# Seven block products over pairs of token tiles in the projections of a linear-attention kernel, and a planned order of the other engines

## The chip, the cores and the metric

The kernel runs on one core of a Trainium2 chip. The metric is the device time of one execution in microseconds; smaller is better. Five engines work side by side, each through its own list of instructions in order: PE (TensorE, matrix products into PSUM banks), DVE (VectorE), ACT (ScalarE), POOL (GpSimd) and SP, which here only issues DMA transfers. An instruction waits on semaphores for what it reads, and for the last reader of what it overwrites.

## The reference

For 2048 tokens of 640 channels, the kernel computes

```
out = x + attention(layernorm(x)) + mlp(layernorm(x))       S = 2048, D = 640
q, k, v   = split(xn @ wqkv)                 32 heads of 20
phi(z)    = [softmax(z @ w_phi), softmax(-z @ w_phi)]        per head, 40 wide
kv, z     = sum over tokens of phi(k)^T v, phi(k)
attention = ((phi(q) kv) / (phi(q) z + 1e-6)) @ wo
mlp       = gelu(xn @ w1 + b1) @ w2 + b2      640 -> 1728 -> 640
```

All of it is float32. The products `q @ w_phi` and `k @ w_phi` are folded into the weights before the projections start, so that one matrix `wkv` (640 x 1344 columns) gives the arguments of the feature maps of k (columns 0 to 639) and of q (640 to 1279), and 64 columns of v; `wv` (512 columns) gives the rest of v.

## The kernel before

A float32 operand is kept as two parts, `hi` (rounded to float32r, a form that PE reads at full speed) and `lo` (the remainder), and a product is three matmuls, hi·hi, hi·lo and lo·hi. ACT writes `hi`, and DVE or POOL subtracts it for `lo` (`split`, L60 and L63).

PE goes through four stages: the MLP of token blocks 0 and 1 (a block is 512 tokens), with the folding of the weights and the transposing of x beside it; the projections of 16 token tiles of 128; the MLP of blocks 2 and 3 with the attention's output beside it; and the end. The change is in the second, and in what runs beside the first.

**A tile of the projections** takes four banks' worth of products (`proj(t, i)`, matmuls at L913): columns 0 to 511 (i = 0), 512 to 1023 (i = 1), the "narrow" bank of 320 columns (i = 2: the last q columns and 64 of v) and the "wide" bank of v (i = 3). Each is five contraction chunks of 128, three matmuls a chunk: 15 matmuls. Three PSUM banks (0 to 2) take turns. The other five hold the sums over all tokens of phi(k)^T v; `kv_tile` (L974, L978, 11 short matmuls) adds the products of tile t-2 to them behind the first bank of tile t. The last of them, of tile 15, stands in the MLP that follows: `last_kv` puts it behind ten steps of that MLP, and these are the 30 matmuls of its first layer for weight chunks 0 and 1. The last order is `TAIL`: both tiles' banks 0 and 1 first, then narrow and wide of 14 and of 15.

**A feature map** (`features`, `k_tile`, `q_tile`; once for k and once for q of each tile) is a chain over three engines: ACT copies the bank to SBUF (L925), DVE takes maximum and minimum per head (L932, L933), POOL makes two differences (L938), ACT the exponentials of both (L939), DVE the sums (L941) and their reciprocals (L947, for q L991), and POOL the product with them (L949 for k, 128x1280; L992 and L995 for q). For k, ACT and DVE then split it (L60, L63: `lo` on DVE, 128x1280) for the products with v; for q, DVE turns it in blocks of 32 (L1001) and SP stores it. v itself goes from its bank to SBUF on ACT (L965, hi) and DVE (L967, lo).

**The order.** PE's list is written out by hand everywhere. In the MLP of blocks 0 and 1 the lists of all engines are as written; the call `order.close()` at L888, ahead of the projections, ends that, and from there the framework's scheduler decides the order in the lists of DVE, ACT, POOL and SP by its own estimates.

Weights of the output (`wo`) are split beside tiles 1, 2, 3, 6 and 7, and the first weights of the next MLP stage beside tiles 12 to 15, on ACT and POOL.

The kernel already has a product by seven blocks instead of eight elsewhere: in the MLP of blocks 2 and 3 (`cross`), which is not changed.

## Time and profile before

| | |
|---|---|
| median of 3 runs | 700.8 us (700.64 to 700.96) |
| profiled execution: its time, its span | 701.24 us, 699.5 us |
| PE busy | 693.6 us, 3331 matmuls |
| DVE, ACT, POOL busy | 523.3, 365.2, 437.9 us |
| MLP of blocks 0 and 1 | span 0 to 211 us |
| projections | 211 to 428 us |
| from there to the last product of `kv_tile` | 428.0 and 436.1 us |

The profiled execution is one of its own and took 0.44 us more than the median of the runs; the 1.74 us between its time and its span lie before the first and behind the last instruction that the profile shows. All times in the trace count from the span's start. A bare matmul of 128x512 here means 512 columns moved through PE with a 128x128 weight. PE is the engine to look at first, since it is busy 99% of the span; the other three have room on the average, but each feature map passes through all of them in turn.

### The profile page before, as it was taken

Reading aid. Unit: us, or ns where it says so; the run is one execution under the profiler, and the core shown is the slowest. Engines: PE = TensorE matmul, PEld = TensorE weight load, DVE = VectorE, ACT = ScalarE, POOL = GpSimd, SP = SyncE. Lnnn points to the kernel's source line nnn. Section 1 sums busy time; section 2 is a strip of 40 time slices with the busy share of each in tenths; the row PEclk is TensorE's granted clock in tenths of the full one; section 3 lists DMA queues with packets and bytes.
Section 4 is the critical chain, followed back from the end, with each engine's and each line's share of the span. In section 5 each row is a group of like instructions: output and inputs, shape, how many; then the busy total and the mean of one; then the engine's idle time right before and its main releaser. Section 6 shows DMA issues by size and latency. Waiting matters only on the chain.

```text
span 699.5 us, 9720 instructions
## 1 busy us (share of the span) xinstructions
PE 693.6 (99%) x3331; PEld 584.8 (84%) x3331; DVE 523.3 (75%) x859; ACT 365.2 (52%) x617; POOL 437.9 (63%) x324
## 2 busy tenths in 40 slices
PE   8999999999999999999999999999999999999998
PEld 7888888888888888888888888888888888888886
DVE  7778654987754787788878888948688686789783
ACT  6434643344433545554544546557676666659350
POOL 3711314566245886687666869648689997577930
PEclk9999999999999999999999999999999999999999
DMA  9834633485634227326500705874355548881222
GB/s 315 256 126 124 198 109 99 158 268 172 210 116 155 81 90 227 93 75 205 136 1 1 189 0 201 284 210 128 111 149 160 184 148 291 287 278 63 76 76 105
DMA packets 67463, 107.61 MB, mean 154 GB/s; under 512 B 7622, under 2 KB 31974, under 8 KB 65790
## 3 DMA queue, kind: packets, MB, share of 16 engines
q1 hardware_dynamic: 67110, 106.98, 48.1%
q8 instruction: 26, 0.43, 0.3%
q14 instruction: 23, 0.19, 0.1%
q10 hardware_dynamic: 304, 0.01, 0.0%
HBM read 72.42 MB, written 34.55 MB: 153 GB/s over the span
## 4 chain that ended last, share of the span: by engine, by line
PE 96%; DVE 2%; DMA 0%; issue 0%; ACT 0%; DVEq 0%
PE bank L913 29%; PE bank L69 19%; PE bank L70 19%; PE bank L71 19%; PE bank L974 3%; PE bank L648 2%; PE bank L1208 1%; PE bank L1209 1%; PE bank L554 1%; PE bank L313 1%; PE bank L332 1%; PE bank L312 1%; PE bank L331 1%; DVE st L137 0%; DMA xb<-in_x 0%; DVE rx L1257 0%
## 5 line engine op out<-in xcount | busy, mean ns | idle before, releaser
L913 PE MATMUL bank<-wkh,y 128*128 128x512 f32 (+1 forms) x480 | 139.8, 365 | 0.0
L69 PE MATMUL bank<-m,w 128*128 128x512 f32 x288 | 113.1, 393 | 0.0
L70 PE MATMUL bank<-m,w 128*128 128x512 f32 x288 | 112.2, 390 | 0.0
L63 POOL TENSOR_TENSOR w<-r,w 128x640 fp32r<-128x640 f32 x32 | 52.6, 1656 | 92.8 <-ACT w L60 62.3
L71 PE MATMUL bank<-m,w 128*128 128x512 f32 x266 | 103.7, 390 | 0.0
L69 PE MATMUL bank<-y,w 128*128 128x512 f32 (+1 forms) x256 | 99.7, 389 | 0.0
L70 PE MATMUL bank<-y,w 128*128 128x512 f32 (+1 forms) x256 | 99.0, 387 | 0.0
L913 PEld LDWEIGHTS bank<-wkh,y 128*128 128x128 f32 x480 | 87.5, 188 | 12.9
L71 PE MATMUL bank<-y,w 128*128 128x512 f32 (+1 forms) x246 | 95.1, 387 | 0.0
L913 PE MATMUL bank<-wkl,y 128*128 128x512 f32 (+1 forms) x240 | 87.1, 363 | 0.0
L69 PEld LDWEIGHTS bank<-m,w 128*128 128x128 f32 x288 | 54.1, 188 | 11.4 <-issue 0.4
L70 PEld LDWEIGHTS bank<-m,w 128*128 128x128 f32 x288 | 54.1, 188 | 10.9
L938 POOL TENSOR_TENSOR m<-m,mx 128x640 f32<-128x640 f32 x32 | 42.1, 1315 | 31.9 <-DVE mx L932 31.8
L939 ACT ACTIVATE m<-m,rs_all 128x1280 f32<-128x1280 f32 x32 | 43.7, 1364 | 30.4 <-POOL m L938 30.4
L71 PEld LDWEIGHTS bank<-m,w 128*128 128x128 f32 x266 | 49.9, 188 | 10.4
L941 DVE TENSOR_REDUCE sm<-m 128x64 f32<-128x1280 f32 x32 | 47.3, 1477 | 13.9 <-ACT m L939 13.7
L336 DVE TENSOR_TENSOR acc<-bank,acc 128x512 f32<-128x512 f32 x70 | 47.3, 684 | 13.6 <-PE bank L71 8.4
L913 PE MATMUL bank<-w,y 128*128 128x512 f32 x240 | 57.4, 391 | 0.0
L69 PEld LDWEIGHTS bank<-y,w 128*128 128x128 f32 x256 | 48.1, 188 | 10.4 <-ACT bank L1276 0.3
L70 PEld LDWEIGHTS bank<-y,w 128*128 128x128 f32 x256 | 48.1, 188 | 9.4
L71 PEld LDWEIGHTS bank<-y,w 128*128 128x128 f32 x246 | 46.2, 188 | 9.4
L949 POOL TENSOR_TENSOR m<-m,w 128x1280 f32<-128x1280 f32 x16 | 39.2, 2448 | 20.4 <-DVE w L947 18.4
(242 smaller groups left out, 1524.7 us busy)
## 6 DMA issues: line engine op xcount, KB each, us to landing
r<-in_w SPq DMA_DIRECT2D x52, 320.0 KB
e<-e SPq DMA_DIRECT2D x40, 256.0 KB
e<-acc SPq DMA_DIRECT2D x52, 160.0 KB
t<-t SPq DMA_DIRECT2D x8, 512.0 KB
acc<-in_xT SPq DMA_DIRECT2D x3, 1280.0 KB
tf<-t SPq DMA_DIRECT2D x2, 1536.0 KB
xb<-in_x SPq DMA_DIRECT2D x8, 320.0 KB
t<-in_x SPq DMA_DIRECT2D x8, 320.0 KB
```

The costliest lines, as they stand in the source:

```text
L63: eng.tensor_tensor(lo, src, f(hi), op=ALU.subtract)
L69: nc.tensor.matmul(ps, lh, rh, start=first, stop=False, **kw)
L70: nc.tensor.matmul(ps, lh, rl, start=False, stop=False, **kw)
L71: nc.tensor.matmul(ps, ll, rh, start=False, stop=last, **kw)
L336: nc.vector.tensor_tensor(acc[b][:, m, :], pw, acc[b][:, m, :], op=ALU.add)
L648: nc.tensor.matmul(ps[:, u * nh * DF:(u + 1) * nh * DF], raw[:nh * DH, u * P:(u + 1) * P], wpt[:nh * DH, g, :nh, 1:], start=True, stop=True)
L913: nc.tensor.matmul(ps, lh[:, kc, c], rh[:, kc], start=n == 0, stop=n == 3 * KC - 1)
L938: subs[n, t] = nc.gpsimd.tensor_tensor(ep[:, :, s], a, b, op=ALU.subtract)
L939: exps[n, t] = nc.scalar.activation(e, e, AF.Exp, scale=rs_all[:, t:t + 1])
L941: nc.vector.tensor_reduce(sm, e.rearrange("p a (h f) -> p (a h) f", f=DH), axis=AX, op=ALU.add)
L949: nc.gpsimd.tensor_tensor(e3, e3, w.unsqueeze(2).to_broadcast([P, 2 * H, DH]), op=ALU.mult)
L974: nc.tensor.matmul(kvp[g // 2][:, (g % 2) * 240:(g % 2) * 240 + 240].rearrange("p (i c) -> p i c", i=2), v[:, g * VS:(g + 1) * VS], ft[:, ...
```

## The change

**Fewer products.** Tiles 2 to 7 are taken in pairs (2,3), (4,5), (6,7). For a pair, the columns 0 to 1023 and the contraction chunks 0 to 3 form a product of 2x2 blocks: two token tiles, two column halves, and two contraction halves (chunk 2q and 2q+1, q = 0 and 1). It is made by seven block products with sums of blocks (a11, a12, a22 are column blocks of `wkv`, b11, b21, b22 blocks of x; s1 to s4 and t1 to t4 are sums of them), in Winograd's form. A block product is six matmuls of 128x512 (two q, three of hi and lo); chunk 4 is added directly, three matmuls for each of the four results ("rest"). A pair so has 7 x 6 + 4 x 3 = 54 matmuls of this shape in place of 4 x 15 = 60.

**Sums in the PSUM.** Partial sums that belong to several results stay in one bank and are added to: a result is first copied to SBUF by ACT while the bank goes on, and what belongs to this result alone is added to it from a second bank by DVE (`move` with `add=True`, L1234). k's arguments of a pair's second tile get a place of their own beside the first's (`pks`, four places: k of either tile, q of either).

**Sums of blocks.** Those of the weights are made by DVE and POOL: of q = 0 beside the MLP stage, of q = 1 in tiles 0 and 1, where all eight are also split (8 ACT, 8 DVE instructions of 128x512). s3 takes the place of columns 512 to 1023 of one chunk of `wkv` in SBUF, which are saved in DRAM before and loaded again in pair (6,7). Those of x (t1 to t4) are made beside the MLP stage from blocks 0 and 1 (`turned_forms`: POOL 8 sums and 8 `lo` parts of 128x512 and 16 differences of 128x256, ACT 8 `hi` parts), stored, and loaded again for each pair (1 MB, SP).

**The order.** All of the projections' instructions on ACT, DVE, POOL and SP are now placed by a planner (`Plan`). Each piece of work has a cost in us, what it waits for, and a rank; at each step it takes the engine whose next piece can start first, and there the piece with the best rank. `lo` of k's features may go to DVE (cost 1.75) or POOL (2.6), whichever comes first (`either`): of 16, 9 come to DVE and 7 to POOL, that of tile 15 among the latter. PE's list is given. When PE's list is empty the planner ends; the pieces left (`over`) are issued behind `order.close()`, and there the framework's scheduler orders them as before. q's factor (L992 of before, on POOL) moves to DVE (L1039). The output's weights are split beside tiles 8 to 10. PE's order in tiles 0 and 1 is (0,0), (0,1), (1,1), (0,2), (0,3), (1,0), (1,2), (1,3).

Three places in the lists follow. The first is POOL around the end of the projections; `m_3897`, `m_3945` and `m_4001` are the features of k of tile 15, q of 14 and q of 15, `m_3847` k of 14, and `w_4048` weights of the next stage. Before:

```order
L949 TENSOR_TENSOR m_3847<-m_3847,w 128x1280
L938 TENSOR_TENSOR m_3945<-m_2044,mx 128x32x20
L938 TENSOR_TENSOR m_3945<-mx,m_2044 128x32x20
L949 TENSOR_TENSOR m_3897<-m_3897,w 128x1280
L63 TENSOR_TENSOR w_4048<-r_3674,w_4048 128x640
L938 TENSOR_TENSOR m_4001<-m_2043,mx 128x32x20
L938 TENSOR_TENSOR m_4001<-mx,m_2043 128x32x20
L63 TENSOR_TENSOR w_4048<-r_3675,w_4048 128x640
L1125 MEMSET kvs 128x1408
```

With the change, where the same three are `m_4080`, `m_4104` and `m_4166`, and `w_4134` the weights:

```order
L1022 TENSOR_TENSOR m_4104<-m_2136,mx 128x32x20
L1022 TENSOR_TENSOR m_4104<-mx,m_2136 128x32x20
L1022 TENSOR_TENSOR m_4166<-m_2136,mx 128x32x20
L1499 TENSOR_TENSOR w_4134<-r_3920,w_4134 128x640
L1022 TENSOR_TENSOR m_4166<-mx,m_2136 128x32x20
L1600 MEMSET kvs 128x1408
L63 TENSOR_TENSOR w_4134<-r_3921,w_4134 128x640
L1044 TENSOR_TENSOR m_4080<-m_4080,w 128x1280
L1047 TENSOR_TENSOR m_4104<-m_4104,w 128x32x20
L1047 TENSOR_TENSOR m_4166<-m_4166,w 128x32x20
L1055 TENSOR_TENSOR w_4152<-m_4080,w_4152 128x1280
```

The product of k of tile 15 (`m_3897` by L949 before, `m_4080` by L1044 now) has moved behind both differences of q of tile 15, the memset and both splits of weights, and its `lo` (L1055, `w_4152`), which was on DVE, is now the last of these rows on POOL.

The second is DVE at the same place. Before (`bank_3959` and `bank_3979` are banks of v of tiles 14 and 15):

```order
L941 TENSOR_REDUCE sm<-m_3897 128x64
L967 SCALAR_TENSOR_TENSOR v_2037<-bank_3959,rs_all,v_2037 128x10x48
L967 SCALAR_TENSOR_TENSOR v_2037<-bank_3959,rs_all,v_2037 128x32
L947 RECIPROCAL w<-sm 128x64
L63 TENSOR_TENSOR w_3856<-m_3847,w_3856 128x1280
L932 TENSOR_REDUCE mx<-m_2043 128x32
L933 TENSOR_REDUCE mx<-m_2043 128x32
```

With the change (`m_2136` the arguments of q of tile 15, `m_4104` the features of q of 14, `bank_4110` wide v of tile 15):

```order
L1030 TENSOR_REDUCE sm<-m_4080 128x64
L1012 TENSOR_REDUCE mx<-m_2136 128x32
L1013 TENSOR_REDUCE mx<-m_2136 128x32
L1089 SCALAR_TENSOR_TENSOR v_2132<-bank_4086,rs_all,v_2132 128x11x12
L1036 RECIPROCAL w<-sm 128x64
L1030 TENSOR_REDUCE sm<-m_4104 128x64
L1089 SCALAR_TENSOR_TENSOR v_2132<-bank_4110,rs_all,v_2132 128x10x48
L1089 SCALAR_TENSOR_TENSOR v_2132<-bank_4110,rs_all,v_2132 128x32
```

The sums of k of tile 15 stand ahead of the extremes of q of 15 as before; their reciprocal is now behind those extremes and behind a part of v.

The third is DVE within pair (4,5), with the change alone (`bank_2603` and `bank_2631` are banks whose sum is added to the arguments):

```order
L1036 RECIPROCAL w<-sm 128x64
L1012 TENSOR_REDUCE mx<-m_2136 128x32
L1013 TENSOR_REDUCE mx<-m_2136 128x32
L1234 TENSOR_TENSOR m_2135<-bank_2603,m_2135 128x32x16
L1055 TENSOR_TENSOR w_2616<-m_2508,w_2616 128x1280
L1030 TENSOR_REDUCE sm<-m_2578 128x64
L1038 RECIPROCAL w<-sm 128x32
L1039 TENSOR_TENSOR w<-sm,w 128x32
L1234 TENSOR_TENSOR m_2135<-bank_2631,m_2135 128x32x3
L1234 TENSOR_TENSOR m_2136<-bank_2631,m_2136 128x32x13
```

The additions from PSUM stand between the pieces of feature maps of the pair before. In the diff, cut to its core, the body of the planner's loop and the steps of the feature maps, which compute what they did, are left out.

```diff
+    def raw_sums(q, ts):
+
+        def block(i, j):
+            return [f(w[:, 2 * q + j, 512 * i:512 * i + 512]) for w in wkv_]
+
+        a, b, c, d = ts
+
+        def joined(o, i, j):
+            return lambda: nc.vector.tensor_tensor(o, *block(i, j), op=ALU.add)
+
+        def made(o, x0, x1, op):
+            return lambda: nc.gpsimd.tensor_tensor(o, x0, x1, op=op)
+
+        return [joined(a, 1, 0), joined(b, 1, 1), made(b, a, b, ALU.add), joined(c, 0, 0), made(a, c, a, ALU.subtract),
+                made(c, b, c, ALU.subtract), joined(d, 0, 1), made(d, d, c, ALU.subtract)]
...
+    def turned_forms():
+
+        for b in range(2):
+            for q in range(2):
+                r = [gp.tile([P, 512], F32, name="xq", bufs=4) for i in range(2)]
+                for o, c in zip(r, (2 * q, 2 * q + 1)):
+                    nc.gpsimd.tensor_tensor(o, *(f(z[:, c]) for z in y[b]), op=ALU.add)
+                    yield 2
+                (r0e, r0o), (r1e, r1o) = ([z.rearrange("p (i j n) -> p i j n", i=2, j=2)[:, :, j] for j in range(2)] for z in r)
+                for n, (o, x0, x1) in enumerate(((r0e, r0o, r0e), (r0o, r1o, r0o), (r1o, r1o, r0e), (r1e, r1e, r1o))):
+                    nc.gpsimd.tensor_tensor(o, x0, x1, op=ALU.subtract)
+                    yield 1 + n % 2
+                for i in range(2):
+                    hi = gp.tile([P, 512], F32, name="xq", bufs=4)
+                    nc.scalar.activation(hi.bitcast(F32R), r[i], AF.Copy)
+                    yield 1
+                    nc.gpsimd.tensor_tensor(r[i].bitcast(F32R), r[i], hi, op=ALU.subtract)
+                    for p, z in enumerate((hi, r[i])):
+                        nc.sync.dma_start(f_dram[b][:, :, q, i, p].rearrange("k p n -> p k n"), z.rearrange("p (k n) -> p k n", k=2))
+                    yield 2
...
+    mlp.beside = both(prep(), late_start(LATE, paced(turned_forms())))
...
+    class Plan:
+
+        def __init__(self):
+            self.ops = []
...
+        def add(self, engine, took, emit, *after, rank=1000):
+
+            return self.either({engine: took}, {engine: emit}, *after, rank=rank)
+
...
+    LANDS, SOON = 4.0, 0.9
...
+        ops = [plan.add("DVE", 1.46, steps[0], *ready, *([before[1]] if before else []), rank=rank)]
+        ops.append(plan.add("POOL", 2.48, steps[1], ops[0], *(e_free[s - 3] if s > 2 else []), *([chains[s - 1][1]] if s else []), rank=rank - 2))
+        p3_free[i] = ops[1]
+        ops.append(plan.add("ACT", 1.27, steps[2], ops[1], rank=rank))
...
+        ops.append(plan.add("DVE", 0.46 if n == "k" else 0.45, steps[4], ops[3], rank=rank))
+        ops.append(plan.add("POOL", 2.35 if n == "k" else 1.27, steps[5], ops[4], rank=rank))
+        if n == "k":
+            hi = plan.add("ACT", 1.19, steps[6], ops[5], rank=rank)
+            lo = plan.either({"POOL": 2.6, "DVE": 1.75}, {"POOL": lambda: steps[7](nc.gpsimd), "DVE": lambda: steps[7](nc.vector)}, hi, rank=rank)
+            ops += [hi, lo]
+            k_done[t], k_hi[t] = [lo], hi
...
+    def move(get, i, j, add, *after, f0=None):
+
+        ops = []
+        parts = [(slice(0, 512), j, 1, 0.58, 0.64)] if i == 0 else [(slice(0, KQ - 512), j, 1 + 512 // H, 0.19, 0.2), (slice(KQ - 512, 512), 2 + j, 1, 0.45, 0.52)]
+        for cols, n, f0, act, dve in parts:
+            def emit(cols=cols, n=n, f0=f0):
+                src = get()[:, cols].rearrange("p (f h) -> p h f", h=H)
+                o = pks[n].rearrange("p (h f) -> p h f", f=DH)[:, :, f0:f0 + src.shape[2]]
+                if add:
+                    nc.vector.tensor_tensor(o, src, o, op=ALU.add)
+                else:
+                    nc.scalar.activation(o, src, AF.Copy)
+            ops.append(plan.add("DVE" if add else "ACT", dve if add else act, emit, *after, *([p3_free[n]] if n in p3_free else []), rank=0))
+        return ops
...
+    def plan_kv(t, i):
+
+        def products():
+            bank(i)
+            psum_of[t, "kx"] = psum[i]
+            kv_products(t, fts.pop(t), vbuf[t % 2], psum[i])
+
+        op = plan.add("PE", 1.22, products, *k_done[t], *v_ready[t], *bank_free[i])
+        kv_done[t] = v_free[t % 2] = op
+        bank_free[i] = (plan.add("DVE", 0.28, lambda: kx_sum(t, psum_of[t, "kx"]), op, rank=1),)
+        if t + 1 in k_hi:
+            k_hi[t + 1][3] = (*k_hi[t + 1][3], op)
...
+        def product(ps, w, yn, first):
+            for q in range(2):
+                for n, (pl, pr) in enumerate(((0, 0), (0, 1), (1, 0))):
+                    nc.tensor.matmul(ps, left(yn, pl, q), right(w, pr, q), start=first and q == 0 and n == 0, stop=False, skip_group_check=True)
...
+        def rest(ps, i, j):
+            for n, (pl, pr) in enumerate(((0, 0), (0, 1), (1, 0))):
+                nc.tensor.matmul(ps, y[b][pl][:, 4, cs[j]], wkv_[pr][:, 4, 512 * i:512 * i + 512],
+                                 start=False, stop=n == 2, skip_group_check=True)
...
+        z = pe(a, "a11", "b11", True)
+        z11 = move(bank_of(a), 0, 0, False, z)
+        z = pe(b1, "a12", "b21", True, rest_of=(0, 0))
+        d11 = move(bank_of(b1), 0, 0, True, z, *z11)
+        bank_free[b1] = tuple(d11)
+        z = pe(a, "s2", "t2", False, *z11)
+        z12 = move(bank_of(a), 0, 1, False, z)
+        z4 = pe(b1, "a22", "t4", True, rest_of=(1, 0))
+        z = pe(a, "s3", "t3", False, *z12)
+        z21 = move(bank_of(a), 1, 0, False, z)
+        d21 = move(bank_of(b1), 1, 0, True, z4, *z21)
+        bank_free[b1] = tuple(d21)
+        plan_features(t, "k", 0, d11[0], d21[0])
+        z = pe(c, "s1", "t1", True)
+        plan.add("PE", 0.0, lambda: next_forms(t))
+        z22 = move(bank_of(c), 1, 1, False, z)
+        z = pe(a, None, None, False, *z21, rest_of=(1, 1))
+        d22 = move(bank_of(a), 1, 1, True, z, *z22)
+        bank_free[a] = tuple(d22)
+        plan_kv(t - 2, b1)
+        z = pe(c, "s4", "b22", False, *z22, rest_of=(0, 1))
+        d12 = move(bank_of(c), 0, 1, True, z, *z12)
+        bank_free[c] = tuple(d12)
+        plan_features(t + 1, "k", 1, d12[0], d22[0])
+        _, q = plan_narrow(t, 0, a)
+        plan_features(t, "q", 2, d21[1], q)
+        plan_wide(t, b1)
+        plan_kv(t - 1, c)
+        _, q = plan_narrow(t + 1, 1, a)
+        plan_features(t + 1, "q", 3, d22[1], q)
+        plan_wide(t + 1, b1)
+
+    def next_forms(t):
+        if t < 6:
+            yts[t + 2] = load_forms(t + 2)
...
+    thirds = plan_sums()
+    for n, (t, i) in enumerate(((0, 0), (0, 1), (1, 1), (0, 2), (0, 3), (1, 0), (1, 2), (1, 3))):
+        plan_part(t, i, n % 3)
+    for op in thirds:
...
+    for t in range(2, 8, 2):
+        if t == 4:
+            plan.add("PE", 0.0, lambda: load_y(2))
+        plan_pair(t)
+    plan.add("PE", 0.0, lambda: load_y(3))
+    n, wo_done = 0, ()
+    for t, i in [(t, i) for t in range(8, 14) for i in range(4)] + TAIL:
+        plan_part(t, i, n % 3)
...
+        tk = {(15, 1): 13, (15, 3): 14}[t, i] if (t, i) in ((15, 1), (15, 3)) else t - 2 if t < 15 and i == (t == 8) else None
         if tk is not None:
...
+            plan_kv(tk, n % 3)
...
+    over = plan.run()
+    order.close()
+    for step in over:
+        step()
```

More of the change, by code (lines that the diff above doesn't have):

```diff
@@ L650, in products, with both, late_start @@
         return us, ps
+    def both(*gens):
+        for _ in zip_longest(*gens):
+            yield
+    LATE = 5
+    def late_start(n, gen):
+        for _ in range(n):
+            yield
+        yield from gen
     jobs = [units[o:o + 2] for o in range(0, 14, 2)]
@@ new lines, in first_weights, with plan_pair_splits, open_w1t @@
+    def first_weights():
+        nonlocal mlp
+        mlp = Mlp((0, 3, 2, 1), ((1, 2), (0, 3)))
+        mlp.ph = ptile
+        mlp.fetch_pair(0, False)
+    def plan_pair_splits(*after):
+        def open_w1t():
+            nonlocal w1t
+            w1t, parts = wp.tile([P, 4, D], F32R, name="w0"), mlp.raw.pop((0, False))
+            raw.extend(parts)
+        raw, done, before = [], [], plan.add("SP", 0.0, lambda: open_w1t(), *after)
+        for j in range(2):
+            hi = plan.add("ACT", 0.66, lambda j=j: nc.scalar.activation(w1t[:, 2 * j], raw[j], AF.Copy), before, rank=400)
+            done.append(plan.add("POOL", 1.5, lambda j=j: nc.gpsimd.tensor_tensor(w1t[:, 2 * j + 1], raw[j], f(w1t[:, 2 * j]), op=ALU.subtract),
+                                 hi, rank=400))
+        return done
@@ new lines, in plan_second_split, with hi @@
+    def plan_second_split(*after):
+        def hi():
+            nonlocal w2t, late
+            w2t, raw = wp.tile([P, 4, D], F32R, name="w3"), mlp.raw.pop((0, True))
+            late = [lambda: split(w2t[:, 2], w2t[:, 3], raw[1], eng=nc.gpsimd)]
+            first.append(raw[0])
+            nc.scalar.activation(w2t[:, 0], raw[0], AF.Copy)
+        first = []
+        a = plan.add("ACT", 0.66, hi, *after, rank=400)
+        plan.add("POOL", 1.5, lambda: nc.gpsimd.tensor_tensor(w2t[:, 1], first[0], f(w2t[:, 0]), op=ALU.subtract), a, rank=400)
```

430 lines of the change are left out of this document (319 added, 111 removed).

## The prediction

> **What bounds the kernel now.** I read first the busy times of the page, then what ends at each step of the chain that ended last, then every wait of PE:
>
> ```profile
> span 699.5 us, 9720 instructions
> PE 693.6 (99%) x3331; PEld 584.8 (84%) x3331; DVE 523.3 (75%) x859; ACT 365.2 (52%) x617; POOL 437.9 (63%) x324
> PE 96%; DVE 2%; DMA 0%; issue 0%; ACT 0%; DVEq 0%
> ```
>
> ```profile
> PE bank L582 <- POOL m L580: 1.3, 1, 1.3
> PE bank L185 <- DVE xb L171: 0.9, 1, 0.9
> PE bank L1208 <- DVE acc L1222: 0.2, 1, 0.2
> ```
>
> PE is 96% of the chain, and its whole list of waits has nothing between the start (L582, L185) and the end (L1208). So in the projections every matmul taken away is worth its whole pitch, and every wait that the change brings is paid in full. The pitch is in the chain itself:
>
> ```profile
> 211.12 28.25 PE bank L913 x135
> 239.37 1.13 PE bank L974 x10
> 240.57 12.52 PE bank L913 x60
> ...
> 405.21 10.29 PE bank L913 x45
> ...
> 416.71 11.30 PE bank L913 x60
> 428.01 1.13 PE bank L974 x10
> ```
>
> The 45 matmuls from 405.21 are all of 512 columns (one wide bank of v is among them, also 512): 10.29 / 45 = 0.2287 us each. The 60 from 416.71 hold 30 of those and 30 narrow ones: (11.30 - 30 x 0.2287) / 30 = 0.148 us. A tile is 45 x 0.2287 + 15 x 0.148 + the products of k and v, 12.52 + 1.20 = 13.72 us.
>
> The windows of the first stage's second part and of the projections show how full the other engines are:
>
> ```profile
> 57.50:113.00 55.50, 55.50 (x285) 47.17 (x285) 37.65 (x91) 26.25 (x53) 12.40 (x8) 1.00 0.51 155
> 211.00:428.00 217.00, 217.00 (x1117) 187.89 (x1116) 172.68 (x256) 107.51 (x166) 157.05 (x117) 1.00 0.34 101
> ```
>
> After the window's length stand the busy times of PE, its weight loads, DVE, ACT and POOL. In the projections DVE has 172.7 of 217 and POOL 157.1; both have room, but little enough that the order in their lists decides when something is ready.
>
> **Term 1, the matmuls.** Six fewer in each of three pairs: 18 x 0.2287 = 4.12 us less. Nothing else on PE is added; the seven products and the rests have the old shape.
>
> **Term 2, the end of the projections.** Let E be the end of the products of (15,3), 428.01 above. From E, PE does the products of k and v of tile 14 (1.20), then 30 matmuls of the MLP, then those of tile 15, which need `lo` of k of tile 15. What leads to it before:
>
> ```profile
> 422.75 1.28 POOL L938 TENSOR_TENSOR m<-m,mx 128x640 f32<-128x640 f32 x1
> 423.99 1.28 POOL L938 TENSOR_TENSOR m<-mx,m 128x640 f32<-128x640 f32 x1
> 425.22 3.62 POOL L949 TENSOR_TENSOR m<-m,w 128x1280 f32<-128x1280 f32 x1
> 428.81 1.57 POOL L63 TENSOR_TENSOR w<-r,w 128x640 fp32r<-128x640 f32 x1
> 430.34 1.27 POOL L938 TENSOR_TENSOR m<-m,mx 128x640 f32<-128x640 f32 x1
> 431.58 2.52 POOL L938 TENSOR_TENSOR m<-mx,m 128x640 f32<-128x640 f32 x1
> 434.06 1.56 POOL L63 TENSOR_TENSOR w<-r,w 128x640 fp32r<-128x640 f32 x1
> 435.57 1.27 POOL L1125 MEMSET kvs<- 128x1408 f32 x1
> ```
>
> ```profile
> 426.54 0.81 DVE L932 TENSOR_REDUCE mx<-m 128x32 f32<-128x640 f32 x1
> ...
> 428.43 1.49 DVE L941 TENSOR_REDUCE sm<-m 128x64 f32<-128x1280 f32 x1
> ...
> 431.11 1.85 DVE L63 TENSOR_TENSOR w<-m,w 128x1280 fp32r<-128x1280 f32 x1
> ```
>
> ```profile
> 436.11 1.13 PE bank L974 x10
> ```
>
> The product of k of 15 begins at 425.22, E - 2.8; ACT makes `hi` of it, and DVE's `lo` ends at 432.96, E + 5.0. PE comes for it at 436.11, E + 8.1. The slack is 3.1 us.
>
> With the change POOL's list has, between the differences of q of 14 and that product, six more rows, and `lo` itself is on POOL. The first of the six, a difference of q of 15, can't begin before DVE has q's maximum (L932). The narrow bank of 15 ends 15 x 0.2287 = 3.43 before E, ACT's copy takes about 0.4 and the maximum 0.81: E - 2.2 at the earliest. On DVE the sums of k of 15 (1.49, behind an exponential that comes after ACT's copies of v) now stand ahead of it as well, and I place the start at E - 1.1. From there POOL is a plain sum of its own means:
>
> ```profile
> L938 POOL TENSOR_TENSOR m<-mx,m 128x640 f32<-128x640 f32 x32 | 43.4, 1355 | 3.1 <-DVE mx L933 3.1
> L938 POOL TENSOR_TENSOR m<-m,mx 128x640 f32<-128x640 f32 x32 | 42.1, 1315 | 31.9 <-DVE mx L932 31.8
> L949 POOL TENSOR_TENSOR m<-m,w 128x1280 f32<-128x1280 f32 x16 | 39.2, 2448 | 20.4 <-DVE w L947 18.4 <-ACT m L925 2.0
> L995 POOL TENSOR_TENSOR m<-m,w 128x640 f32<-128x640 f32 x16 | 20.4, 1277 | 1.3
> L63 POOL TENSOR_TENSOR w<-r,w 128x640 fp32r<-128x640 f32 x4 | 6.3, 1572 | 0.0
> ```
>
> First difference 1.32, a split 1.57, second difference 1.36, memset 1.27, split 1.57, product of k 2.45, two products of q 2 x 1.28, and `lo`. That of 128x1280 on POOL isn't in the trace; 2.45 (the product of that size) and 2 x 1.57 = 3.14 (the split of half the size, twice) bound it, and I take the middle, 2.8. Sum 14.9, so `lo` ends at E - 1.1 + 14.9 = E + 13.8, and PE, there at E + 8.1, waits **5.7 us**. The bounds: with the start at E - 2.2 and `lo` at 2.45, 4.2; with `lo` at 3.14 and one product of 3.62 and one difference of 2.52 as in the rows above (1.2 more each), 8.4. Behind the waiting products on PE's list stands all of the MLP, so all of the wait is paid; POOL's and ACT's work there waits for nothing from PE that could give it back.
>
> A smaller wait lies within that one: the MLP's first product takes the bank that wide v of 15 had. DVE's `lo` of that v now comes behind the sums of k of 15 and of q of 14 and a reciprocal, about E + 2.7, while PE wants the bank at E + 1.2. PE loses 1.5 there and as much less at the second place. If the wait for k were gone, 1.5 would stay.
>
> **Term 3, waits in the pairs.** Before, a bank had two banks' time (over 5 us) to be emptied. In a pair the same bank is used again after one product in between, 6 matmuls or 1.37 us (9 or 2.06 with a rest): ACT must copy it, or DVE add it, within that. The rows of the same size:
>
> ```profile
> L925 ACT ACTIVATE m<-bank 128x512 f32<-128x512 f32 x16 | 10.1, 628 | 16.9 <-PE bank L913 9.7 <-issue 6.9
> L336 DVE TENSOR_TENSOR acc<-bank,acc 128x512 f32<-128x512 f32 x55 | 37.2, 685 | 12.1 <-PE bank L71 8.4 <-PE bank L332 3.3
> L63 DVE TENSOR_TENSOR w<-m,w 128x1280 fp32r<-128x1280 f32 x16 | 28.5, 1782 | 18.2 <-ACT w L60 18.2
> ```
>
> A copy (0.63) fits. An addition (0.69) fits unless it stands behind a long piece of a feature map: behind a whole `lo` it would be 1.78 + 0.69 - 1.37 = 1.1 late. In the list such a `lo` stands behind the first addition and ahead of the others, where PE is past the tight place. I take 0.3 us for all three pairs; the bounds are 0 and 3 x 1.1 = 3.3. By the same walk k and v's products come late nowhere: k of t-2 is ready since the pair before.
>
> **Term 4, what is added beside other work: 0.** In the MLP stage POOL gets 8 sums and 8 `lo` of 128x512, 16 differences of 128x256 and 4 sums of weights; by these rows
>
> ```profile
> L63 POOL TENSOR_TENSOR w<-t,w 128x512 fp32r<-128x512 f32 x1 | 1.3, 1304 | 0.0
> L393 POOL TENSOR_TENSOR m<-r 128x256 f32<-128x256 f32 x1 | 0.8, 790 | 1.4 <-DMA r<-in_w 1.4
> ```
>
> 20 x 1.3 + 16 x 0.79 = 38.7 us, in a window where POOL is busy 12.4 of 55.5 and the weights' folding is what it would delay. Without that cover it would be paid in full. DVE gets 4 sums of weights there. In tiles 0 and 1 DVE has 12 more instructions of 0.69 (8.3 us) and ACT 8 of 0.63, in each pair DVE has some 3.0 of additions, and it sheds the `lo` of five tiles (8.9) to POOL: about 97 of 104 us in tiles 0 to 7, full but not over. The loads of x's sums, 1 MB in a pair of 26 us, are issued a pair ahead, and the DMA share in the projections' window is 0.34; the stores and loads of one chunk's columns are smaller.
>
> **Sum.** 701.24 - 4.12 + 5.7 + 0.3 = 703.1 for a profiled execution. That of before lay 0.44 above its median, so 702.7 us.
>
> **The rivals.** What a measurement can tell from no change here is about 0.2%, or 1.4 us: faster is below 699.4, slower above 702.2.
>
> *The waiting PE comes back at half speed.* PE would stand still for 1.5 and then some 4.2 us, where before it never stands. At the start it runs slowly after a pause:
>
> ```profile
> 1.31 5.83 PE L582 MATMUL bank<-m 128*128 128x512 f32 x18 [1.31 <-POOL m L580]
> ```
>
> ```profile
> 4.70 2.44 PE L582 MATMUL bank<-m 128*128 128x512 f32 x10
> ```
>
> The first 8 took (4.70 - 1.31) / 8 = 0.424 us each and the next 0.24. If a pause does that, 3.4 us at half speed cost 1.7: 704.4. The Trainium skill states such a rule ("TensorE: Matmul & The Clock Gate", Part 1): an idle window of about 3.4 us brings the clock to half, and about 3.4 us of sustained matmuls bring it back; the rows of the start agree with the second half, and no run here shows the first. The windows being free-running by that page, a pause of 4 us need not fill one. Against it: two pieces of the pause are apart. Chance 0.14.
>
> *POOL is ahead of my list, and k arrives in time.* Not slower. The wait is gone if `lo` ends by E + 8.1, 5.7 earlier than I have it; the change breaks even where it ends 1.6 earlier (E + 12.2). The place is the first of the six rows: if DVE's maximum of q of 15 comes at E - 2.2 and POOL has done a part of the list's other rows (the splits, the memset) in gaps before, it decides. For it: the pieces behind `order.close()` are ordered by the framework's estimate of the same durations, and the 3.62 and 2.52 of before may be exceptions. Against: the list is fixed as it stands in the order, eight rows can't take less than their means by much, and no gap comes before the first. The bank's 1.5 us would stay: 701.24 - 0.44 - 4.12 + 0.3 + 1.5 = 698.5, and 697.0 without it. Chance 0.24.
>
> *The pairs don't keep pace.* DVE's additions or the copies come late at each of the tight places: three places per pair, three pairs, at up to 1.1, are 9.9 at the worst and half of that as a mean, 3.3 + 1.6 over the tail's 5.7: 706. It decides from an addition that stands behind more than 0.69 us of other work on DVE. For it: 97 of 104 us. Against: the planner gives additions the first rank. Chance 0.12.
>
> **How the numbers follow.** The forecast (the tail's wait, 701.2 to 705.4 by its bounds) has 0.50, the clock 0.14, the early arrival 0.24, the pairs 0.12. Slower: 0.31 of the forecast's 0.50, the clock and the pairs, 0.57. Same: the forecast's lower end, 0.19, and a late form of the early arrival, 0.03, together 0.22. Faster: the other 0.21 of the early arrival. The range goes from 697.4, within the early arrival, to 706.0, the pairs; the forecast's own is the one just named.
>
> **What would show it.** PE's waits have one new long row, the products of tile 15 of k and v (L1103) on POOL's `lo` (L1055), near 5 us, and a short one of the MLP's first product on DVE's v (L1089). From the first product of the projections to those of tile 14 it is 217.0 - 4.1 us; more means that the pairs wait, in rows on L1234. The matmuls after the long wait at 0.42 instead of 0.23 are the clock. I am wrong if POOL's product of k (L1044) begins before E + 4, or if no wait on L1055 is there.

## The result: slower by 8.7 us

The changed kernel takes 709.5 us (median of 4, 709.2 to 710.6) against 700.8 before: a ratio of 1.0127, 95% interval 1.0109 to 1.0145. 702.7 with a range to 706.0 had been forecast; the sign was right and the size was less than a quarter of what came.

The page of the changed kernel, and the longer of PE's waits that the kernel before hasn't:

```profile
span 707.4 us, 9858 instructions
PE 693.7 (98%) x3313; PEld 582.6 (82%) x3313; DVE 549.6 (78%) x902; ACT 373.5 (53%) x633; POOL 496.3 (70%) x355
```

```profile
PE bank L1103 <- POOL w L1055: 4.1, 1, 4.1
PE bank L69 <- DVE v L1089: 1.5, 1, 1.5
PE bank L69 <- DVE acc L338: 1.3, 3, 0.6
...
PE bank L70 <- DVE y L700: 0.9, 2, 0.6
PE bank L1103 <- DVE w L1055: 0.4, 1, 0.4
```

PE has its 18 matmuls less (3313 for 3331), and is busy as long as before (693.7 for 693.6 us): some of its matmuls were slower. The two spans, 699.5 and 707.4, are divided by setting the same PE instruction of both traces side by side at four places:

| stretch | before | after | difference |
|---|---|---|---|
| start to the first product of the projections | 210.96 | 214.65 | +3.7 |
| from there to the products of k and v of tile 14 | 216.89 | 213.32 | -3.6 |
| from there to those of tile 15 | 8.10 | 13.96 | +5.9 |
| from there to the 1000th matmul from the end | 35.43 | 37.10 | +1.7 |
| the rest | 228.1 | 228.4 | +0.3 |

The second line is the gain that was forecast, 4.12, less one wait of 0.4 (L1103 on DVE, tile 13). The third is the two waits of the end that were forecast. The first and the fourth are the error.

**The pairs.** The chain of waits in pair (2,3):

```profile
239.65 2.72 PE bank L1334 x12
242.37 0.68 PE bank L1338 x3
...
252.49 0.70 PE bank L1338 x3
```

Its 54 matmuls, and the products of k and v among them, follow one another from 239.65 to 253.19 without a gap, at 0.227 us each (2.72 / 12). No row of PE's waits is on L1234: all of DVE's additions came in time.

**The end of the projections.** POOL's timeline:

```profile
427.04 1.28 POOL L1022 TENSOR_TENSOR m<-m,mx 128x640 f32<-128x640 f32 x1 [0.68 <-DVE mx L1012]
...
433.95 2.37 POOL L1044 TENSOR_TENSOR m<-m,w 128x1280 f32<-128x1280 f32 x1
...
438.98 2.89 POOL L1055 TENSOR_TENSOR w<-m,w 128x1280 fp32r<-128x1280 f32 x1
```

E, the start of the products of tile 14, is 427.97 here. The first difference starts at E - 0.9 (E - 1.1 forecast) and `lo` ends at 441.87, E + 13.9 (E + 13.8). Behind the wait PE is slow:

```profile
441.93 1.75 PE L1103 MATMUL bank<-w,v 128*128 128x240 f32 x10 [4.08 <-POOL w L1055]
...
444.13 0.63 PE L70 MATMUL bank<-y,w 128*128 128x512 f32 x1
444.56 0.63 PE L71 MATMUL bank<-y,w 128*128 128x512 f32 x1
...
446.24 0.40 PE L69 MATMUL bank<-y,w 128*128 128x512 f32 x1
```

The starts are 0.43 us apart up to 446.2 and 0.23 after it, and the ten products of k and v took 1.75 where they took 1.29 before. That is the rival of the clock, at 1.7 us. The trace's record of the granted clock agrees: it goes to 0.50 at 442.78 and back to 1.00 at 446.19, 3.41 us later. In these windows PE's busy time stands first behind the length, and the granted clock third from the end:

```profile
439.36:442.78 3.42, 0.85 (x7) 0.85 (x8) 3.27 (x6) 1.18 (x4) 2.52 (x1) 1.00 0.92 286
442.78:446.19 3.41, 3.41 (x12) 2.91 (x12) 2.94 (x8) 2.48 (x7) 2.64 (x4) 0.50 0.99 221
```

**The first stage.** The window from 57.5 to 113 us:

```profile
57.50:113.00 55.50, 55.27 (x291) 47.13 (x290) 38.73 (x89) 31.59 (x64) 38.68 (x34) 1.00 0.71 216
```

Most of POOL's added work is there, as expected (38.7 us busy, 12.4 before), and PE, busy for 55.27 of the 55.50, was hardly idle. The losses, read from how far each of PE's instructions falls behind its like of before, stand at 40 to 46 us (2.2 us), at 93 (0.5), at 141 and at 169 (0.7 each); PE had been 0.4 ahead till then. DVE and POOL at the first of them:

```profile
37.87 1.78 DVE L700 TENSOR_TENSOR y<-xb,y 128x512 fp32r<-128x512 f32 x1
39.57 0.68 DVE L338 TENSOR_TENSOR acc<-bank,acc 128x512 f32<-128x512 f32 x1
40.17 1.16 DVE L696 TENSOR_TENSOR xb<-xb,m 128x512 f32<-128x512 f32 x1
41.25 1.23 DVE L700 TENSOR_TENSOR y<-xb,y 128x512 fp32r<-128x512 f32 x1
```

```profile
37.36 3.42 POOL L887 TENSOR_TENSOR xq<-y,y 128x512 f32<-128x512 f32 x2
40.73 4.68 POOL L891 TENSOR_TENSOR xq<-xq 128x256 f32<-128x256 f32 x4
```

The sums of x begin at 37.4, as soon as POOL is free and their inputs (block 0) exist, and not in the window from 57.5 us on, by which Term 4 had been worked out. DVE is then writing y of block 1, which PE's MLP takes next. L700 and L696, with both operands in SBUF, take up to 1.78 us beside POOL; L338, which reads PSUM, keeps its 0.68.

### The profile page after: what moved, and what is told of

The parts are those of the page before. It is cut to its first block, busy times and chain, and to the rows that moved or that the text cites. A ratio compares the mean times of both kernels' runs of the same rounds, so it can differ in the third digit from the quotient of the medians.

```text
span 707.4 us, 9858 instructions
## 1 busy us (share of the span) xinstructions
PE 693.7 (98%) x3313; PEld 582.6 (82%) x3313; DVE 549.6 (78%) x902; ACT 373.5 (53%) x633; POOL 496.3 (70%) x355
## 4 chain that ended last, share of the span: by engine, by line
PE 76%; DVE 10%; DMA 5%; POOL 4%; issue 2%; ACT 1%; SPq 0%; POOLq 0%; DVEq 0%; ACTq 0%
PE bank L990 17%; PE bank L69 15%; PE bank L70 15%; PE bank L71 14%; PE bank L1334 4%; PE bank L1103 2%; DMA r<-in_w 2%; DVE acc L338 1%; PE bank L1683 1%; DMA f<-xq 1%; PE bank L1684 1%; PE bank L650 1%; PE bank L1338 1%; POOL m L1022 1%; DVE xq L800 1%
## 5 line engine op out<-in xcount | busy, mean ns | idle before, releaser
L990 PE MATMUL bank<-wkh,y 128*128 128x512 f32 (+1 forms) x360 | 101.4, 355 | 0.0
L990 PEld LDWEIGHTS bank<-wkh,y 128*128 128x128 f32 x360 | 65.0, 188 | 8.2
L63 POOL TENSOR_TENSOR w<-r,w 128x640 fp32r<-128x640 f32 x29 | 47.6, 1656 | 33.0 <-ACT w L60 28.3
L990 PE MATMUL bank<-wkl,y 128*128 128x512 f32 (+1 forms) x180 | 63.6, 354 | 0.0
L990 PE MATMUL bank<-w,y 128*128 128x512 f32 x240 | 57.5, 391 | 0.0
L338 DVE TENSOR_TENSOR acc<-bank,acc 128x512 f32<-128x512 f32 x70 | 47.1, 683 | 11.8 <-PE bank L71 6.2
L1677 POOL TENSOR_TENSOR e<-e,m 128x512 fp32r<-128x512 f32 x28 | 41.7, 1490 | 16.3 <-ACT m L1676 16.2
L990 PEld LDWEIGHTS bank<-w,y 128*128 128x128 f32 x240 | 44.4, 188 | 8.5
```

The costliest lines, as they stand in the source:

```text
L63: eng.tensor_tensor(lo, src, f(hi), op=ALU.subtract)
L338: nc.vector.tensor_tensor(acc[b][:, m, :], pw, acc[b][:, m, :], op=ALU.add)
L990: nc.tensor.matmul(ps, lh[:, kc, c], rh[:, kc], start=n == 0, stop=n == 3 * KC - 1)
L1677: mlp.after(1, lambda: nc.gpsimd.tensor_tensor(pl, e, f(ph), op=ALU.subtract))
```

## The experiments

Each ratio is to runs of the kernel before on the same chip (medians 700.8 to 701.0).

### The sums of x later, by program order

```diff
-    LATE = 5
+    LATE = 18
```

> One number of the changed kernel is altered: the sums of x (t1 to t4) begin 13 ticks of the MLP later (LATE 5 to 18, a tick being three matmuls, 0.7 us), so that POOL's first sums and differences no longer run at 37 to 45 us, where DVE writes y of block 1. Theory (POOL's work slows DVE's instructions beside it, there from 0.68 to 1.2 and 1.8 us, and PE waits for y): the products of the projections begin at 212.6 us instead of 214.8, and the time is 2.2 less than the changed kernel's 709.5, 707.3 (706.8 to 707.8). Rival (what costs is the work itself, its stores and its share of POOL, wherever it stands): 709.5, within 0.5.

710.0 us, ratio 1.0127 (1.0110 to 1.0144): no gain, the projections begin at 215.4. The edit didn't do what it was for, and told two things by that. POOL's first sum has nothing ahead of it in its list, and ran at 37.5 as before; only the second came later. One POOL instruction beside DVE so stands alone here:

```profile
37.47 1.73 POOL L887 TENSOR_TENSOR xq<-y,y 128x512 f32<-128x512 f32 x1
```

```profile
37.97 1.77 DVE L700 TENSOR_TENSOR y<-xb,y 128x512 fp32r<-128x512 f32 x1
39.67 0.68 DVE L338 TENSOR_TENSOR acc<-bank,acc 128x512 f32<-128x512 f32 x1
...
40.87 0.68 DVE L700 TENSOR_TENSOR y<-xb,y 128x512 fp32r<-128x512 f32 x1
```

It makes one L700 1.1 us longer, all behind it are 0.68, and PE's first wait (0.7 at 40.4) is there, while those at 44 to 46 are gone. In their place the wait at 141 us grows from 0.5 to 1.0, and the folding's matmuls wait:

```profile
PE bank L650 <- PE bank L650: 0.7, 1, 0.7
PE bank L650 <- DMA raw<-in_wqT: 0.7, 1, 0.7
```

### The sums of x later, by their inputs

```diff
-        for b in range(2):
-            for q in range(2):
+        for b in (1, 0):
+            for q in (b, 1 - b):
...
-                for o, c in zip(r, (2 * q, 2 * q + 1)):
+                for o, c in ((r[1], 2 * q + 1), (r[0], 2 * q)):
```

> The changed kernel with the sums of x made in another order: block 1 before block 0, and of block 1 chunk 3 first. The first sum on POOL so reads a part of y that DVE writes at about 43 us, and has to wait for it; nothing else on POOL, DVE, ACT and PE moves. Theory (one POOL instruction beside DVE's makes the latter 1.1 us longer, and PE's waits at 40 to 46 us come from that): those waits (0.6, 0.65, 0.2 and the slower first matmuls behind each) go, the projections begin at 212.6 instead of 214.8, and the time is 707.3 (706.8 to 707.9). Rival (the stores of the sums hold up the loads behind them in SP's queue, so a later start is paid at 84 to 95 us, as in the run with LATE 18): 709 to 710, with waits of the folding's matmuls (L650) there.

708.6 us, ratio 1.0108 (1.0094 to 1.0122). POOL now waits for DVE, and DVE is done almost before it:

```profile
42.30 3.00 POOL L887 TENSOR_TENSOR xq<-y,y 128x512 f32<-128x512 f32 x2 [4.83 <-DVE y L700]
```

```profile
41.54 0.68 DVE L700 TENSOR_TENSOR y<-xb,y 128x512 fp32r<-128x512 f32 x1
...
42.75 1.40 DVE L700 TENSOR_TENSOR y<-xb,y 128x512 fp32r<-128x512 f32 x1
```

The waits at 40 to 46 are gone, and the projections begin at 212.56, 2.1 earlier, as the theory had it (212.6). That the total fell by 0.9 only is due to the end: the granted clock is 0.50 there for 6.83 us in this profile, for 3.41 in that of the changed kernel.

### The sums of weights of q = 0 later as well

```diff
-            events.append((9 + 8 * n, len(events), step, ()))
+            events.append((106 + 3 * n, len(events), step, ()))
```

(with LATE 18)

> As the run with the later sums of x, and the sums of weights of q = 0 (4 on DVE, 4 on POOL) also moved, behind the scaling of blocks 2 and 3 (from tick 9 + 8n to 106 + 3n). Theory: the small waits of PE at 141 and 169 us (0.5 and 0.2, each with the slower first matmuls behind it) go too, the projections begin at 211.1 to 211.7 and the time is 705.9 to 706.5. Rival (they were not what made DVE late there, or they are in the way at the new place): 707.3, like the run before it.

708.2 us, ratio 1.0102 (1.0085 to 1.0119), 1.8 below the run with LATE 18 alone, 0.8 to 1.4 having been expected of this step. Its only trace is of an execution of 991 us at a granted clock of 0.66, which can't be set beside the others, so where the 1.8 lies isn't shown. The run with the sums of x ordered by their inputs has no wait at 141 either, with the sums of weights at their old place, and 0.2 left at 167. The first combined kernel below has the changes of both in this stage; its projections begin at 211.65, 0.9 before those of the run with the sums of x alone.

### The planned order without the seven products

Tiles 2 to 7 are made by `plan_part` like the others; `plan_sums`, `turned_forms`, the sums of q = 0 and the stores of saved columns are left out.

> The changed kernel without the seven products: tiles 2 to 7 as the others, four banks of 15 matmuls, no sums of x or of weights; the planned order, the moved splits of wo and the leftover pieces stay. Theory: the 18 matmuls come back (+4.1), the waits in the MLP go (-3.7), the end of the projections stays as it is (wait of 5.6 and 2.0 of half speed): 708.4 to 709.6, with the projections beginning at 211.1. Rival (part of the loss around the end comes from work that the pairs push back): the wait at the end is shorter by over 1 us, 707 or less. Rival (the planned order itself makes PE wait elsewhere): over 711.

708.8 us, ratio 1.0105 (1.0088 to 1.0122). The projections begin at 210.5, so all of the first stage's loss belongs to the sums of blocks. Most of the end's loss belongs to the planned order: from the products of tile 14 to those of tile 15 it takes 12.8 us without a single product saved, against 14.0 with the change and 8.1 before, and the slow stretch is there as well. The other 1.1 comes with the pairs, as the first rival had it, though its time (707 or less) didn't.

```profile
PE bank L1098 <- POOL w L1050: 3.4, 1, 3.4
...
PE bank L1098 <- DVE w L1050: 1.1, 2, 0.9
PE bank L69 <- DVE kxa L1108: 1.0, 1, 1.0
```

The planned order also makes PE wait 1.1 within the projections (0.9 of it for tile 13). So the seven products as they stand, with what feeds them, were worth nothing: between the two profiles the projections are 5.1 shorter with them, the first stage is 4.2 longer, the end 1.1 and the rest 0.3.

### The leftover pieces by hand

```diff
-            rest = {n: (op, e) for e in left for n, op in left[e]}
+            rest = {n: (op, e) for e in ("PE", "ACT", "POOL", "DVE", "SP") for n, op in left[e]}
...
     over = plan.run()
+    for n in (12, 5, 13, 6, 0, 14, 1, 2, 3, 7, 4, 8, 9, 10, 11, 15):
+        over[n]()
     order.close()
-    for step in over:
-        step()
```

The first line is why `lo` of tile 15 was on POOL: a piece that may go to either engine and is left over stands in the lists of both, and the later list, POOL's, won.

> The changed kernel with only the 16 pieces that the planner left over in another order: they are issued by hand ahead of the end of the ordered part, the product of k of tile 15 ahead of the differences of q of 15 on POOL, its lo on DVE. Theory (POOL's order made k late, and the pause of 4.1 us brought the half-speed stretch of 4 us behind it): the wait on lo goes, the slow matmuls go with it, and the bank's wait of 1.5 stays at 0.5 to 1.5: 709.5 - 4.2 - 2.0 - (0 to 1.0) = 702.3 to 703.3. Rival (the half speed came from something else than the pause): 704.3 to 705.3. Rival (something other than POOL makes lo of tile 15 late, ACT's hi behind the gelu or v): the wait stays over 2 us, 706 or more.

705.7 us, ratio 1.0067 (1.0052 to 1.0082): 3.9 below the changed kernel, where 6.2 to 7.2 was expected. `lo` is in time, and no product of k and v of 15 waits. But the wait for v's bank has grown, because the list by hand puts q's extremes ahead of v on DVE, and the slow stretch came behind that one:

```profile
PE bank L69 <- DVE v L1089: 2.3, 1, 2.3
```

```profile
431.42 0.58 PE L69 MATMUL bank<-y,w 128*128 128x512 f32 x1 [2.32 <-DVE v L1089]
...
434.79 0.52 PE L71 MATMUL bank<-y,w 128*128 128x512 f32 x1
435.14 0.40 PE L69 MATMUL bank<-y,w 128*128 128x512 f32 x1
```

### Only the engine of `lo`

The first line of the last diff alone.

> The changed kernel with one thing altered: of the leftover pieces lo of k of tile 15 goes to DVE, and POOL's order stays, with the product of k of 15 at its late place. Worked out from the changed kernel's rows: hi on ACT ends at 438.4 behind the gelu, lo on DVE at 440.3, and PE, there at 437.9, waits 2.4 instead of 4.1. Theory (a pause of over 2 us is enough for the half speed, as in the run with the leftover pieces by hand): 709.5 - 1.7 = 707.8 (707.3 to 708.3), with matmuls of 0.43 behind the pause. Rival (only a pause near 4 us does that to this place): 705.8. Rival (lo's engine is all of the wait): below 704.

709.1 us, ratio 1.0107 (1.0090 to 1.0125). The wait on `lo` is 2.5 (2.4 expected), so POOL's late product is the larger part, and `lo`'s engine 1.5. The slow stretch stays (442.2 to 445.8). The time fell by 0.4 and not by 1.7, since the profiled execution lost another 2.0 us at the folding's products (the projections begin at 216.7 in it):

```profile
PE bank L1103 <- DVE w L1055: 2.5, 1, 2.5
...
PE bank L650 <- DMA raw<-in_wqT: 0.9, 1, 0.9
```

The folding's waits are not steady with the sums of x: three kernels that are alike up to there, the changed one, the one by hand and this one, wait 0.2, 0.1 and 2.0 us at L650 in their profiles; what they wait for wasn't isolated. Of four executions of this kernel three took 708.7 to 709.5, and one 706.0. That one had a mean granted clock of 1.00, and so no slow stretch, which is 1.7 of its difference.

### The slow stretch in the kernel before

```diff
     def last_kv():
-        for _ in range(10):
+        for _ in range(0):
             yield
```

> The kernel before, with the products of k and v of tile 15 put 3 matmuls behind the MLP's start instead of 30. lo of that k ends at 432.96, so PE, there at 429.9, must pause some 3.1 us, in a kernel without any of the change. Theory (a pause of over 2 us brings about 4 us of half speed): 701.0 + 3.1 + 2.0 = 706.1. Rival (the half speed of the changed kernel has another cause, its POOL or DMA work): 704.1, matmuls at 0.23 behind the pause.

706.8 us, ratio 1.0085 (1.0066 to 1.0103). No part of the change is in this kernel:

```profile
432.65 2.49 PE L974 MATMUL bank<-w,v 128*128 128x240 f32 x10 [3.05 <-DVE w L63]
...
438.94 0.40 PE L69 MATMUL bank<-y,w 128*128 128x512 f32 x1
```

A pause of 3.05 us is followed by slow matmuls up to 438.9, 6.3 us of them (the granted clock is 0.50 from 432.0 to 438.8). A pause alone is enough for it; nothing of the change is needed.

### All that was found, together

Four kernels, each with one step more. The first has the sums of x by their inputs, the sums of weights late, the leftover pieces by hand, and the MLP's first product on the bank of the narrow products of 15:

```diff
+    ptile.n = 2
     mlp.beside = last_kv()
```

> All that the runs so far point to, together: the sums of x in the order that waits for y, the sums of weights of q = 0 behind the scaling of blocks 2 and 3, the leftover pieces by hand with lo of k of tile 15 on DVE, and the MLP's first product put on the bank that the narrow products of tile 15 left, not on that of wide v. Theory: the wait on v goes too, and with it the half-speed stretch behind it (the pause of 2.3 us had one as well); what is left of the changed kernel's losses is 0.4 on k of tile 13 and some 0.5 in the MLP: 701.0 - 4.1 + 0.9 = 697.8 (697.2 to 698.6). Rival (the MLP's waits only move, as with LATE 18): 699 to 702. Rival (v or the sum of tile 14 holds up another bank): a wait of PE over 1 us stays at the MLP's first or second product, 700 or more.

704.8 us, ratio 1.0055 (1.0042 to 1.0069). The end is clear, the products of tile 15 stand 8.1 us behind those of 14 as before, and the next piece is late: the split of the second matrix, which the hand list had put last.

```profile
PE bank L71 <- POOL w L1499: 3.4, 1, 3.4
```

So the rival was right that another wait takes the place, though at a later product than it said. In the profiled execution (702.6) no slow stretch followed this pause; the other four took 703.5 to 705.4, at mean granted clocks of 0.995 to 0.997, which fits one or two such stretches.

The second moves that split ahead:

```diff
-    for n in (12, 5, 13, 6, 0, 14, 1, 2, 3, 7, 4, 8, 9, 10, 11, 15):
+    for n in (12, 5, 13, 6, 15, 0, 14, 1, 2, 3, 7, 4, 8, 9, 10, 11):
```

> As the last combined kernel, with one piece moved: the lo of the second matrix's weights (POOL, L1499) stands directly behind the differences of q of tile 15, not as the last of the leftover pieces, since PE's second layer waited 3.4 us for it. Theory (the end of the projections then has no wait over 1 us, and so no half speed in any execution): 697.6 to 698.8, a spread of under 1 us between the executions. Rival (POOL has too much to do at that place whatever its order, and another piece is late): a new wait of PE of 1 us or more on POOL, 700 or more.

700.2 us, ratio 0.9989 (0.9981 to 0.9998): faster than the kernel before by a little, and 1.4 above the highest time expected. The rival's reason, a new wait on POOL, isn't there. Of the waits that the kernel before hasn't, the two longest are L1631 behind the token sums and tile 13 (a third is 0.4 at L650):

```profile
PE bank L1631 <- DVE km L1615: 0.9, 1, 0.9
PE bank L1103 <- DVE w L1055: 0.5, 1, 0.5
```

The third and fourth let PE come later to these two: tile 13 behind (14,2), and L1631 two steps later.

```diff
-        tk = {(15, 1): 13, (15, 3): 14}[t, i] if ...
+        tk = {(14, 2): 13, (15, 3): 14}[t, i] if ...
...
             yield
+        yield
+        yield
         tp = pxt()
         for c, d in ((0, slice(0, 30)), ...
```

> As best2, and PE takes the products of k and v of tile 13 one narrow bank later (behind (14,2), not behind (15,1)). Theory: the wait of 0.4 to 0.5 on lo of k of 13 goes and nothing takes its place, 0.4 below best2. Rival (the later products hold back v or k of tile 15, which wait for them): equal to best2 or slower, with a wait at the products of tile 14 or 15.

> As best3, and PE takes the three short products behind the token sums of k and v (L1631), for which it waited 0.9 us on DVE, two steps of the MLP (6 matmuls, 1.4 us) later. Theory (the wait was all that this place cost): 1.0 below best3, 698.2 to 698.6, and 2.4 below the kernel before. Rival (the attention that follows comes later by the same and PE waits there): equal to best3, with a new wait behind 450 us.

699.4 us, ratio 0.9985 (0.9977 to 0.9994), and 699.05 us, ratio **0.9976 (0.9967 to 0.9985)**, 1.8 us below the kernel before. The steps were 0.8 where 0.4 was expected and 0.35 where 1.0 was; both waits are gone. The last has these waits, all but the second as before the change:

```profile
PE bank L584 <- POOL m L582: 1.3, 1, 1.3
PE bank L650 <- PE bank L650: 0.5, 1, 0.5
PE bank L1689 <- DVE acc L1703: 0.2, 1, 0.2
```

And the same mending without the seven products:

> The planned order without the seven products (four banks of 15 matmuls in every tile, no sums of x or weights), with the mended end of the projections as in best2. It measures the seven products alone, by its difference to best2. Theory: 701.0, within 0.6 of the kernel before (18 matmuls more than best2, 4.1, less best2's remaining waits in the MLP and at tile 13, about 0.9). Rival (the planned order has a gain of its own): below 700.

702.7 us, ratio 1.0032 (1.0019 to 1.0045). It is 2.4 us above best2, which is what the seven products are worth net of their sums. Between the two profiles, 2.7 apart, the projections are 3.9 shorter with them, the first stage is 0.8 longer and what follows the projections 0.3. It is 1.8 above the kernel before, where 701.0 was expected: the planned order has a loss of its own, of which the wait at L1618 (the same as L1631 above) is 1.0 in the profile. The rest of it wasn't looked into, nor why three of its eleven executions took 704.6 to 706.6, at mean granted clocks of 0.995 to 0.998.

## Why the prediction was wrong

- **Term 1, 4.12 us**: right. 3.6 came through, and 0.4 of the rest is the wait of tile 13, which the planned order has without the products too.
- **Term 2, 5.7 us**: right, 5.9 measured, with start, end and both of its parts (1.5 and 4.1) at the forecast values. It wasn't luck: POOL's rows follow one another as they were added up, and the middle taken for `lo` of 128x1280 on POOL, 2.8, measured 2.89.
- **Term 3, 0.3 us**: right for the banks of the pairs (no wait). Its sentence that "k and v's products come late nowhere" was wrong by 0.4.
- **Term 4, "what is added beside other work: 0"**: this failed; it measured 3.7. The step counted POOL's room and named the weights' folding as the cover. What it left out is that POOL's work makes DVE's work beside it longer, and that this work starts when its inputs are there. Of the 3.7, 2.1 went when the sums of x were made to start later, and 0.9 more in the kernel that also moved the sums of weights; the 0.7 that the last kernel keeps, most of it the wait at L650, stays open. That POOL slows DVE could be read in the trace of before, in DVE's groups from 30 to 47 us, where y's `lo` (L687 there) takes 0.90 in the mean and the sums from PSUM 0.68. One of the five takes 1.78, while POOL's L681 is at work up to 38.1; the other four, behind that, take 0.68:

```profile
L687 DVE TENSOR_TENSOR y<-xb,y 128x512 fp32r<-128x512 f32 x5 | 4.5, 900 | 0.0
L336 DVE TENSOR_TENSOR acc<-bank,acc 128x512 f32<-128x512 f32 x5 | 3.4, 679 | 0.0
```

  The Trainium skill has the rule: on the page "SBUF — State Buffer", section "Who interferes with whom", a DVE instruction with two SBUF inputs contends with a GpSimd instruction that reads SBUF, and one with at most one such input, outside the modes that use two ports, doesn't; the rows of L700 (1.78 against 0.68) and L338 (0.68 throughout) agree. Weighed against the change it would have asked which of DVE's rows beside the new POOL work PE waits for.
- **The clock rival**, 0.14: it came true, at 1.7 us in the profiled execution (1.7 forecast), on top of the forecast and not in its place. The argument against it, that the pause is in two pieces, carried nothing: the piece of 4.1 us was enough. Forecast, clock and 3.7 make 708.1, and the medians lie 0.8 further apart than the two profiled executions do (7.9): the profile of the changed kernel is its fastest execution, that of before its slowest.
- **The early arrival** (0.24) and **the pairs** (0.12) didn't come: POOL took its list at its means, and no wait is on an addition.
- **Two sums** don't come out of their own terms. Term 4's DVE time in tiles 0 to 7, "about 97 of 104 us", would be 86: 77.6 busy from 211 to 315 us before, with 8.3 and three times 3.0 more and 8.9 less; the changed kernel has 92.3 in that stretch. And the pairs' 4.9 us in place of 0.3 would give 707.3, not 706, which was the upper end of the range; what came, 709.5, lies above both.

## What to carry to other kernels

Work that is added to an engine with room is hidden only if it doesn't slow an instruction of another engine that something waits for; look at the rows that run beside it, not at the busy shares. An in-order engine starts a piece when its inputs are there: to have it later, it needs a later input, not a later place in the program. Where PE never pauses, a pause of over 2 us can cost its own length and some 1.7 or 3.4 us more, so a list that ends in leftover pieces deserves an order of its own.

## What had not been expected of the hardware

- **The granted clock goes by fixed stretches of 3.41 us.** In thirteen traces all changes of the granted clock in one trace lie whole multiples of 3.41 us apart, and where this grid lies differs from execution to execution. A pause counts by how much of one stretch it fills. All seven stretches behind the start with 2.3 us of idle PE or more (2.32 to 3.41) were followed by a stretch at 0.50; none with 1.7 or less was, if the clock was at 1.00. So the pause of 2.32 in the run by hand, which lies whole in one stretch, brought half speed, and that of 3.35 in the first combined kernel, which falls half on one and half on the next, didn't:

```profile
440.13:443.54 3.41, 1.74 (x8) 1.12 (x6) 2.99 (x7) 1.90 (x3) 1.60 (x3) 1.00 0.79 275
443.54:446.95 3.41, 1.73 (x8) 1.43 (x9) 2.63 (x7) 0.63 (x1) 1.63 (x1) 1.00 0.33 55
```

  In two of the seven the pause reached 0.4 and 0.6 us into the slow stretch, and a second one followed, 6.83 us in all; in the other five PE was never idle in it, and one was all. An estimate from these lengths: half speed for 3.41 us costs 1.7, for 6.83 it costs 3.4. The executions of one kernel differ in the same way: of the changed kernel's four, three have a mean granted clock of 0.998 (709.2 to 709.5 us) and one of 0.994 (710.6). The Trainium skill ("TensorE: Matmul & The Clock Gate", Part 1) gives a free-running window of about 3.4 us, and the record agrees. It asks for an idle one; the measurement decides, and 2.32 idle of 3.41 was enough here.
- **Loads behind stores.** With the sums of x, their stores stand in SP's queue ahead of the folding's loads. Before, and in the last kernel:

```profile
91.26 0.35 SPq L639 DMA_DIRECT2D raw<-in_wqT  x1
```

```profile
90.68 2.57 SPq L899 DMA_DIRECT2D f<-xq  x2
93.35 1.12 SPq L641 DMA_DIRECT2D raw<-in_wqT  x1
```

The load is issued 2.1 us later, right behind the stores, the second of which waited for POOL. It isn't what PE waits for at L650 in this kernel: that wait, of 0.5, ends at 91.78, before the load is issued. The other kernels with these sums wait 0.1 to 0.8 us at this place; what for stays open.
